# Sparse-attention, dense layer and capacity-routed experts: expert loads, splits and routing products put into a fixed sequence

## The chip, the cores and the metric

The kernel runs on one core of a Trainium2 chip. Its time is the device time of one execution, in microseconds (us). TensorE (PE) does matrix products, VectorE (DVE) and ScalarE (ACT) elementwise work, GpSimd (POOL) elementwise work and indirect transfers, SyncE (SP) starts most transfers. Each engine runs its own instructions in the order in which they stand in the program and waits on semaphores for the others.

## The reference, cut to what matters

Three parts follow one another: causal sparse attention (4 x 8 heads, 576 positions, 64 wide), a dense layer (512 to 2048 to 512 with a leaky ReLU), and an expert layer on its output `x` (2304 tokens, 512 wide). The change touches only the last:

```python
logits = x @ w_gate                       # 2304 x 8
order = np.argsort(-logits.flatten())
for idx in order:                         # greedy, by falling logit
    tok, e = (int(idx) // E, int(idx) % E)
    if assigned[tok] >= 0 or counts[e] >= cap:   # cap = 288
        continue
    assigned[tok] = e
    counts[e] += 1
for e in range(E):
    mask = assigned == e
    h = np.maximum(x[mask] @ w1[e], 0.0)
    out[mask] = h @ w2[e]
```

Every expert gets exactly 288 tokens. `w1[e]` is 512 x 1024 and `w2[e]` 1024 x 512, in float32.

## The kernel before, in words

Float32 products are made of three faster ones: each operand is split into a high part (`hi`, rounded by ACT) and the rest (`lo`, a subtraction on POOL or DVE), and hi x hi, hi x lo, lo x hi are added up in PSUM.

Attention and the first dense product come first, then `second(4)` and `second(5)`: the last two of six 384-token blocks of the second dense product (products `q`). Its rows go to a DRAM array `x2d`.

**Routing** is the generator `routes`. For each expert it has a *search* and a *list*. The search (`search`) finds the expert that fills up next and the value of its last token, in five rounds. A round compares all 2304 keys with 128 or 64 thresholds on DVE (masks `G`; rounds 0 and 3 need two), counts on PE with 18 tiny products (`cnt`), turns counts into flags on DVE (`flag`) and adds these up with one product (`tot`), whose result the next round's `G` reads. So a round is a chain DVE, PE, DVE, PE. The search ends with some thirty small DVE operations and a product `po`. The list (`tokens`) makes the expert's 288 token numbers: three one-hot masks `OQ`, `rhs`, 18 products `pi`, and `idx`. All DVE work of routing goes through the helper `Soon` and carries its line, L641.

**An expert** (`expert`) has 32 steps of 6 products `g`: 16 steps for `w1` (8 outputs `hh` by ACT and `hl` by DVE) and 16 for `w2` (4 outputs `ot`, turned back by `pot` and scattered to `out` by POOL). After every second step the routing generator moves on by one yield. `weights(k)` loads eight pieces of 512 KB (`raw`, three buffers) and splits them (`whi` on ACT, `wlo` on POOL, or on DVE for pieces 1, 5, 7). `gather(k)` fetches 288 rows of `x2d` by three indirect transfers on POOL (`xg`); PE turns them (`pet`, 12 transposes), ACT and DVE split them (`exh`, `exl`).

The order on each engine is set by a list scheduler that goes by priority and its own durations; `Soon` raises the priority of routing. In the old kernel, search k+1 and list k+1 both run during experts k-1 and k, and the gather is emitted at step 22 of expert k.

Of the kernel before, what the change touches and what calls it, by code (L numbers as in the profile page):

```python
# [7 lines left out]
F32 = mybir.dt.float32  # L8
# [18 lines left out]
def body(ctx, tc, q, k, v, w_in, w_out, w_gate, w1, w2, out):  # L27
# [617 lines left out]

    def search():
# [16 lines left out]
        for r in range(len(th)):  # L663
# [24 lines left out]
            if r in (0, 2):  # L688
                tb = rbank([128, 16], "tot")
            nc.tensor.matmul(tb[:, 8:9], units[unit][:J], f[:J], start=(r in (0, 2)), stop=True,  # L690
                             skip_group_check=True)
# [20 lines left out]
    def route(k):  # L712
# [20 lines left out]
        nc.tensor.matmul(po, tri, tot, start=True, stop=False)  # L733
# [13 lines left out]
        yield from tokens(k)  # L747

    def tokens(k):
# [4 lines left out]
        soon.scalar_tensor_tensor(s, c1[:, 0], -96.0, s, op0=OP.mult, op1=OP.add)  # L754
        soon.scalar_tensor_tensor(s, c1[:, 1], -96.0, s, op0=OP.mult, op1=OP.add)
        soon.tensor_scalar(cc[:, 0], c1[:, 0], -1.0, 1.0, op0=OP.mult, op1=OP.add)
        soon.tensor_copy(cc[:, 2], c1[:, 1])
        soon.tensor_sub(cc[:, 1], c1[:, 0], cc[:, 2])
        soon.tensor_scalar(s, s, -1.0, None, op0=OP.add)
        OQ = rtile([128, 18, 96], "OQ", BF, bufs=1)  # L760
        for i in range(0, 18, 6):
            soon.tensor_tensor(OQ[:, i:i + 6], jf[:, None, :96].to_broadcast([128, 6, 96]),
                               s[:, i:i + 6].unsqueeze(2).to_broadcast([128, 6, 96]), op=OP.is_equal)
        rhs = rtile([128, 2, 3, 18], "rhs", BF)
        soon.tensor_mul(rhs[:, 0], cc, jf[:, None, :18].to_broadcast([128, 3, 18]))
        soon.tensor_scalar(rhs[:, 1], cc, tokp, None, op0=OP.mult)
        for _ in range(4):
            yield
        pi = rbank([96, 2, 3], "pi")
        for i in range(18):  # L770
            nc.tensor.matmul(pi.rearrange("p t c -> p (t c)"), OQ[:, i], rhs[:, :, :, i].rearrange("p t c -> p (t c)"),
                             start=(i == 0), stop=(i == 17))
# [10 lines left out]
    def weights(k):  # L783
        e = nc.values_load(EXP[k][0:1, 0:1], engines=[mybir.EngineType.SP], min_val=0, max_val=7)
        W[k] = []
        for n in range(8):
            raw = POOLA[0].tile([128, 1024], F32, name="raw", tag="raw", bufs=3)
            if n < 4:
                nc.sync.dma_start(raw, w1[bass.ds(e, 1), 128 * n:128 * n + 128, :].rearrange("e p m -> (e p) m"))
            else:  # L790
                nc.sync.dma_start(raw.rearrange("p (j m) -> p j m", j=2),
                                  w2[bass.ds(e, 1), 256 * (n - 4):256 * (n - 4) + 256, :].rearrange(
                                      "e (j p) m -> p (e j) m", j=2))
            if n < 4 and k % 2:
                hi, lo = (xa.tile([128, 1024], F32R, name="w" + x, tag=f"WI{n + y}") for x, y in (("hi", 0), ("lo", 4)))
            else:
                pool, tag, bufs = (POOLB[0], "w2", 5) if n >= 4 else (POOLA[0], "w1", 4)
                hi = pool.tile([128, 1024], F32R, name="whi", tag=tag + "h", bufs=bufs)
                lo = pool.tile([128, 1024], F32R, name="wlo", tag=tag + "l", bufs=bufs)
            nc.scalar.activation(hi, raw, AF.Copy)  # L800
            (nc.vector if n in (1, 5, 7) else nc.gpsimd).tensor_sub(lo, raw, hi.bitcast(F32))  # L801
            W[k].append((hi, lo))
            yield
# [23 lines left out]
    def expert(k):  # L827
# [41 lines left out]
        def end():  # L869
            back(3, ots[3])  # L870
            put()
# [110 lines left out]
```

## Time and profile before

| what | us |
|---|---|
| three runs | 922.45, 928.96, 1975.76 |
| their median | 928.96 |
| the profiled execution | 926.83 |
| its span in the trace | 925.1 |
| PE busy in it | 860.2 (93%) |
| DVE, ACT, POOL busy | 563.3, 441.9, 471.5 |
| mean granted PE clock | 0.963 |

The page cuts the span into slices; here stretches of the expert stage are used instead, cut at each expert's first product `g` (at 627.68, 662.9, 697.05, 734.65, 773.05, 814.95, 856.5 and 885.55 us; expert 7 ends at 912.4). The last product `q` ends at 613.98. Matmuls overlap, so a busy PE is not a PE at its peak; of the clock, 1.00 is 2.4 GHz and 0.50 is 1.2 GHz.

### The profile page before, as it was taken

What the parts mean: (1) busy time and instruction counts of PE and PEld (TensorE: products, weight loads), DVE (VectorE), ACT (ScalarE), POOL (GpSimd) and SP (SyncE); (2) the same over time, 40 slices, a digit from 0 to 9 for tenths busy, and PEclk for the clock granted to TensorE, in tenths of its full rate; (3) what the DMA queues carried; (4) which work ended last, traced back from release to release, by engine and by line L of the source; (5) the groups of instructions that cost most, each with busy time, mean ns of one, the idle gap of its engine ahead of it and who ended that gap; (6) DMA issues with size and microseconds to landing.
All of it is one profiled execution on the core that took longest, in us unless ns stands there. A gap on an engine that the chain in (4) does not pass through costs nothing.

```text
span 925.1 us, 16905 instructions
## 1 busy us (share of the span) xinstructions
PE 860.2 (93%) x6274; PEld 726.1 (78%) x6274; DVE 563.3 (61%) x1543; ACT 441.9 (48%) x1095; POOL 471.5 (51%) x394
## 2 busy tenths in 40 slices
PE   7889998899999999999999999978998989897994
PEld 4777766587887888778898877658998989797994
DVE  6777889856446445554555556566877767675330
ACT  5778667464446445454455423324435434243531
POOL 3645646564555556555655445745446263426621
PEclk9789999999999999999999999987999999798997
DMA  8596554320111100100000002325356362425710
GB/s 183 142 200 157 141 144 124 119 61 5 36 26 53 43 14 2 47 1 1 35 1 1 1 1 80 114 67 177 129 154 185 102 182 95 141 92 154 213 35 26
DMA packets 86450, 80.59 MB, mean 87 GB/s; under 512 B 65376, under 2 KB 65376, under 8 KB 86368
## 3 DMA queue, kind: packets, MB, share of 16 engines
q1 hardware_dynamic: 78688, 53.30, 21.1%
q0 software_dynamic: 7680, 26.22, 9.3%
q8 instruction: 49, 0.80, 0.4%
q14 instruction: 33, 0.27, 0.1%
HBM read 70.06 MB, written 9.44 MB: 86 GB/s over the span
## 4 chain that ended last, share of the span: by engine, by line
PE 64%; DMA 10%; DVE 9%; issue 7%; POOL 4%; ACT 4%; SPq 1%; POOLq 0%; ACTq 0%; DVEq 0%
PE p L373 5%; PE p L397 5%; DMA raw<-in_moe_w_dram 4%; PE p L375 4%; PE p L374 4%; PE p L399 4%; PE p L398 4%; PE g L859 3%; PE g L860 3%; PE g L861 3%; PE p L536 2%; PE q L896 2%; PE p L538 2%; PE pS L166 2%; PE p L537 2%
## 5 line engine op out<-in xcount | busy, mean ns | idle before, releaser
L352 POOL TENSOR_TENSOR lo<-WO,hi 128x512 fp32r<-128x512 f32 x96 | 126.6, 1319 | 95.1 <-ACT hi L349 94.9
L352 POOL TENSOR_TENSOR lo<-WI,hi 128x512 fp32r<-128x512 f32 x96 | 126.9, 1323 | 90.1 <-DVE hi L351 58.3
L801 POOL TENSOR_TENSOR wlo<-raw,whi 128x1024 fp32r<-128x1024 f32 x40 | 95.8, 2410 | 113.9 <-ACT whi L800 113.3
L373 PE MATMUL p<-xh,hi 128*128 128x384 f32 x256 | 98.1, 383 | 5.5 <-DVE g L382 5.5
L349 ACT ACTIVATE hi<-WO 128x512 fp32r<-128x512 f32 x96 | 60.5, 630 | 88.2 <-PE q L898 43.7
L375 PE MATMUL p<-xh,lo 128*128 128x384 f32 x256 | 86.9, 339 | 1.4 <-POOL lo L352 1.4
L800 ACT ACTIVATE whi<-raw 128x1024 fp32r<-128x1024 f32 x64 | 66.1, 1055 | 44.4 <-DMA raw<-in_moe_w_dram 39.2
L374 PE MATMUL p<-xl,hi 128*128 128x384 f32 x256 | 86.6, 338 | 0.6 <-DVE xl L234 0.6
L397 PE MATMUL p<-hi,gh 128*128 128x512 f32 x192 | 82.8, 431 | 0.8 <-ACT gh L383 0.8
L859 PE MATMUL g<-hh,whi 128*128 128x288 f32 x256 | 81.4, 319 | 0.5 <-ACT hh L843 0.5
L860 PE MATMUL g<-hl,whi 128*128 128x288 f32 x256 | 79.0, 309 | 0.1
L861 PE MATMUL g<-hh,wlo 128*128 128x288 f32 x256 | 78.7, 307 | 0.0
L836 PE MATMUL g<-exh,whi 128*128 128x288 f32 x256 | 78.4, 307 | 0.0
L837 PE MATMUL g<-exl,whi 128*128 128x288 f32 x256 | 77.4, 303 | 0.0
L838 PE MATMUL g<-exh,wlo 128*128 128x288 f32 x256 | 77.2, 302 | 0.0
L399 PE MATMUL p<-hi,gl 128*128 128x512 f32 x192 | 75.7, 394 | 1.3 <-DVE gl L384 1.3
L159 ACT ACTIVATE sc<-sc,mx 96x128 f32<-96x128 f32 (+2 forms) x176 | 67.6, 386 | 16.6 <-DVE mx L157 16.6
L398 PE MATMUL p<-lo,gh 128*128 128x512 f32 x192 | 75.2, 392 | 0.0
L373 PEld LDWEIGHTS p<-xh,hi 128*128 128x128 f32 x256 | 48.2, 188 | 16.6 <-DVE g L382 6.8
L181 POOL TENSOR_TENSOR sc<-sc,mx 96x384 f32<-96x384 f32 (+2 forms) x64 | 52.3, 834 | 17.3 <-DVE mx L179 10.2
L381 ACT ACTIVATE g<-p 128x384 f32<-128x384 f32 x64 | 31.1, 486 | 57.0 <-PE p L375 56.7
L351 DVE CAST hi<-WI 128x512 fp32r<-128x512 f32 x59 | 26.8, 454 | 46.1 <-PE p L374 35.9
(203 smaller groups left out, 2257.5 us busy)
## 6 DMA issues: line engine op xcount, KB each, us to landing
raw<-in_moe_w_dram SPq DMA_DIRECT2D x64, 512.0 KB
wraw<-in_moe_w_in_dram POOLq DMA_DIRECT2D x16, 512.0 KB
wraw<-in_moe_w_out_dram POOLq DMA_DIRECT2D x16, 512.0 KB
rawq<-in_q_dram SPq DMA_DIRECT2D x32, 144.0 KB
rawk<-in_k_dram SPq DMA_DIRECT2D x32, 144.0 KB
x2d<-x SPq DMA_DIRECT2D x18, 256.0 KB
vt<-in_v_dram SPq DMA_DIRECT2D x16, 160.0 KB
vt<-in_v_dram SPq DMA_DIRECT2D x48, 27.0 KB
```

Source lines behind the costliest of these rows:

```text
L352: nc.gpsimd.tensor_sub(lo, src, hi.bitcast(F32))
L373: nc.tensor.matmul(p1, wh[:, cs], xh[:, c], start=(c == 0), stop=False)
L374: nc.tensor.matmul(p1, wh[:, cs], xl[:, c], start=False, stop=False)
L375: nc.tensor.matmul(p1, wl[:, cs], xh[:, c], start=False, stop=(c == 3))
L397: nc.tensor.matmul(p2[t], gh[:, s], oh, start=(f == 0), stop=False)
L398: nc.tensor.matmul(p2[t], gh[:, s], ol, start=False, stop=False)
L399: nc.tensor.matmul(p2[t], gl[:, s], oh, start=False, stop=(f == 15))
L801: (nc.vector if n in (1, 5, 7) else nc.gpsimd).tensor_sub(lo, raw, hi.bitcast(F32))
L836: nc.tensor.matmul(p, wh, xh[:, c], start=(c == 0), stop=False)
L859: nc.tensor.matmul(p, wh, hh[:, j], start=(j == 0), stop=False)
L860: nc.tensor.matmul(p, wh, hl[:, j], start=False, stop=False)
L861: nc.tensor.matmul(p, wl, hh[:, j], start=False, stop=(j == 7))
```

## The change

Four things.

1. `pin(x)` marks an instruction so that it keeps the program's order on its engine against other marked ones. Marked are the first product of each `cnt` and `pi` group, `tot`, the first `po`, `whi`, `wlo`, the gathers, and the first transpose of each `pet` group.
2. `weights` becomes `load(k, n)` and `halves(k, n)`, called at the eight steps of `CH`. A split follows its load three places later; `raw` has four buffers; piece 1 is split on POOL, no longer on DVE.
3. The list of expert k runs beside the search for k+1 (`routes`), in more and smaller steps, and a search gets 11 yields (one more in round 0). Searches are done (`FOUND`) ahead of the first load of an expert, lists (`LISTED`) ahead of the gather, which is emitted at step 16; its transposes stand at steps 24, 26, 28, 30.
4. Four pieces of expert 0 are split within `second(5)`; the rest follow.

```diff
@@ search
                 if i0 == 0:
                     yield
+                    if r == 0:
+                        yield
                 for i in range(i0, i1):
-                    nc.tensor.matmul(cnt[:J], G[:, i - i0], C[:, i], start=(i == 0), stop=(i == 17))
+                    x = nc.tensor.matmul(cnt[:J], G[:, i - i0], C[:, i], start=(i == 0), stop=(i == 17))
+                    if i == i0:
+                        pin(x)
...
@@ route / tokens
-        yield from tokens(k)
...
@@ weights -> load, halves
+    def load(k, n):
+        if n == 0:
+            W[k] = []
+            REG[k % 2] = nc.values_load(EXP[k][0:1, 0:1], engines=[mybir.EngineType.SP], min_val=0, max_val=7)
+        e = REG[k % 2]
+        raw = POOLA[0].tile([128, 1024], F32, name="raw", tag="raw", bufs=4)
...
+    def halves(k, n):
+        raw = RAWE.pop((k, n))
...
+        pin(nc.scalar.activation(hi, raw, AF.Copy))
+        pin((nc.vector if n in (5, 7) else nc.gpsimd).tensor_sub(lo, raw, hi.bitcast(F32)))
...
@@ gather
-            with tc.high_priority(2000):
-                nc.gpsimd.indirect_dma_start(out=xg[:, c], out_offset=None, in_=x2d[:, :],
-                                             in_offset=ind(IDX[k][:, c:c + 1]))
+            pin(nc.gpsimd.indirect_dma_start(out=xg[:, c], out_offset=None, in_=x2d[:, :],
+                                             in_offset=ind(IDX[k][:, c:c + 1])))
+        yield
...
@@ routes
-        for k in range(8):
-            yield from route(k)
-            ROUTED[0] = k + 1
+        T = iter(())
+        for k in range(8):
+            if k == 7:
+                for _ in T:
+                    yield
+            for _ in route(k):
+                if k and next(T, 1) == 1:
+                    LISTED[0] = k
+                yield
+            for _ in T:
+                yield
+            LISTED[0] = k
+            FOUND[0] = k + 1
+            T = tokens(k)
...
@@ the loop over experts
+    CH = {n: i for i, n in enumerate((1, 4, 7, 10, 14, 18, 22, 26))}
...
+            if n in CH:
+                c = CH[n]
+                if c < 3:
+                    halves(k, 5 + c)
+                elif k < 7:
+                    halves(k + 1, c - 3)
+                if k < 7:
+                    need(FOUND, k + 1)
+                    load(k + 1, c)
+            if k < 7:
+                if n == 16:
+                    need(LISTED, k + 1)
+                    nxt = gather(k + 1)
+                    next(nxt)
+                if n >= 24 and n % 2 == 0:
+                    next(nxt, None)
```

On DVE, the first two rounds of the search for expert 3 stood like this before, during expert 1 (`st` is the routing state, `f` the flags' sum):

```order
L641 SCALAR_TENSOR_TENSOR G<-th_5951,zero_5963,st 128x1152 x2
L844 SCALAR_TENSOR_TENSOR hl<-g_7563,hh 128x288
L641 TENSOR_SCALAR flag,f_7553<-cnt 128x8
L844 SCALAR_TENSOR_TENSOR hl<-g_7591,hh 128x288
L641 SCALAR_TENSOR_TENSOR G<-th_5953,tot,st 128x1152
L844 SCALAR_TENSOR_TENSOR hl<-g_7627,hh 128x288
L801 TENSOR_TENSOR wlo<-raw,whi 128x1024
L641 TENSOR_SCALAR flag,f_7617<-cnt 64x8
```

And now, during the last quarter of expert 0:

```order
L641 SCALAR_TENSOR_TENSOR G<-th_5951,zero_5963,st 128x1152 x2
L641 TENSOR_SCALAR c_7288<-st 128x18 x2
L641 SCALAR_TENSOR_TENSOR st<-c_7288,st 128x18
L641 TENSOR_SCALAR flag,f_7353<-cnt 128x8
L641 SCALAR_TENSOR_TENSOR st<-c_7288,st 128x18
L641 TENSOR_SCALAR st<-st 128x18
L641 TENSOR_SCALAR st<-c_7288 128x18
L641 COPY st<-c_7288 128x18
L641 TENSOR_TENSOR OQ<-jf,st 128x576
L641 SCALAR_TENSOR_TENSOR G<-th_5953,tot,st 128x1152
L641 TENSOR_TENSOR OQ<-jf,st 128x576 x2
L641 TENSOR_SCALAR flag,f_7415<-cnt 64x8
```

The list of expert 2 now stands between a round's flags and the next round's masks, and two of its `OQ` ahead of the following flags.

On PE, the same place now (the first `tot` is that of round 0; between the two marks stand the other products of round 1):

```order
L698 MATMUL tot<-f_7353,units_5957 128x1
L888 MATMUL g_7437<-hl,whi 128x288
L889 MATMUL g_7437<-hh,wlo 128x288
L689 LDWEIGHTS G
L689 MATMUL cnt<-C,G 64x8
...
L698 LDWEIGHTS units_5959
L698 MATMUL tot<-f_7415,units_5959 128x1
L838 MATMUL pet<-ident,xg 128x96 x3
L689 LDWEIGHTS G
```

Before, 14 products `g` stood between that `tot` and the next `cnt`; now 2 do, and between the following `tot` and `cnt` three transposes.

On POOL, the middle of the expert stage before:

```order
L801 TENSOR_TENSOR wlo<-raw,whi 128x1024 x5
L875 DMA out_dram<-o,idx 2304x512 x3
L809 DMA xg<-x2d,idx 96x512 x3
L801 TENSOR_TENSOR wlo<-raw,whi 128x1024 x4
L875 DMA out_dram<-o,idx 2304x512 x3
```

And now:

```order
L827 DMA xg<-x2d,idx 96x512 x3
L821 TENSOR_TENSOR wlo<-raw,whi 128x1024 x3
L869 DMA out_dram<-o,idx 2304x512 x3
L821 TENSOR_TENSOR wlo<-raw,whi 128x1024 x3
L827 DMA xg<-x2d,idx 96x512 x3
```

The pattern repeats for every expert: gather, three splits, scatter, three splits.

## Rows read from the trace of the kernel before

**Rows 1.** Busy time by stretch, expert stage: start, us, engines' busy (instructions), PEclk, DMA, GB/s.
```profile
613.98:627.68 13.70, 5.03 (x69) 4.33 (x67) 6.41 (x17) 4.06 (x6) 7.79 (x7) 0.65 0.46 144
627.68:662.90 35.22, 34.68 (x292) 33.55 (x291) 26.04 (x70) 16.08 (x29) 13.47 (x7) 0.89 0.44 136
662.90:697.05 34.15, 33.32 (x316) 31.41 (x315) 25.98 (x69) 14.79 (x28) 17.70 (x12) 1.00 0.50 159
697.05:734.65 37.60, 34.50 (x334) 32.52 (x333) 27.88 (x69) 15.79 (x29) 17.59 (x12) 1.00 0.48 144
734.65:773.05 38.40, 35.55 (x332) 33.69 (x331) 27.34 (x68) 16.06 (x29) 18.62 (x12) 0.96 0.47 141
773.05:814.95 41.90, 37.20 (x304) 35.19 (x303) 27.67 (x73) 15.90 (x28) 17.11 (x12) 0.88 0.40 130
814.95:856.50 41.55, 34.91 (x288) 33.50 (x287) 27.57 (x85) 15.14 (x28) 19.63 (x15) 0.92 0.47 141
856.50:885.55 29.05, 28.47 (x218) 28.00 (x217) 10.13 (x15) 15.07 (x29) 15.79 (x9) 1.00 0.57 172
885.55:912.40 26.85, 26.85 (x206) 26.82 (x205) 6.24 (x9) 6.78 (x17) 4.86 (x4) 1.00 0.08 23
```

**Rows 2.** Waits of PE, 627.7 to 913 us: total, times, longest.
```profile
PE pet L819 <- DMA xg<-x2d,idx: 7.1, 2, 4.2
PE cnt L683 <- DVE G L641: 4.5, 4, 2.4
PE pi L771 <- DVE rhs L641: 3.3, 4, 1.6
```

**Rows 3.** Busy time by stretch, after the longest of these waits.
```profile
843.40:850.20 6.80, 5.39 (x27) 5.34 (x28) 1.70 (x5) 1.78 (x5) 3.80 (x2) 0.50 0.78 194
```

**Rows 4.** DVE by line, 627.7 to 856.5 us: busy, mean ns, idle before.
```profile
L801 DVE TENSOR_TENSOR wlo<-raw,whi 128x1024 fp32r<-128x1024 f32 x19 | 31.4, 1654 | 5.2 <-ACT whi L800 5.2
L641 DVE SCALAR_TENSOR_TENSOR G<-th,tot,st 128x1152 bf16<-128x1152 f32 x19 | 26.5, 1414 | 4.2 <-PE tot L690 4.2
...
L641 DVE TENSOR_TENSOR OQ<-jf,st 128x576 bf16<-128x576 f32 x18 | 12.5, 748 | 0.1
...
L641 DVE SCALAR_TENSOR_TENSOR idx<-ip 96x3 int32<-96x3 f32 x6 | 4.1, 676 | 0.0
...
L641 DVE TENSOR_SCALAR_CACHE_REDUCE flag<-cnt 64x8 bf16<-64x8 f32 x14 | 2.2, 157 | 9.2 <-PE cnt L683 8.6 <-PE g L838 0.6
L641 DVE SCALAR_TENSOR_TENSOR st<-c,st 128x18 f32<-128x18 f32 x12 | 2.1, 179 | 0.1
```

**Rows 5.** The chain that ended last: start, us, what.
```profile
614.63 2.74 DMA x2d<-x
...
648.47 0.66 PE cnt L683 x18
...
661.57 0.80 PE pi L771 x18
```

**Rows 6.** PE in order of time, expert 3: start, us, engine, line, idle before.
```profile
750.14 0.30 PE L859 MATMUL g<-hh,whi 128*128 128x288 f32 x1
750.28 0.29 PE L860 MATMUL g<-hl,whi 128*128 128x288 f32 x1
753.01 0.38 PE L683 MATMUL cnt<-C,G 128*128 128x8 bf16 x9 [2.44 <-DVE G L641]
```

**Rows 7.** POOL in order of time, a gather in expert 4.
```profile
791.77 2.39 POOL L801 TENSOR_TENSOR wlo<-raw,whi 128x1024 fp32r<-128x1024 f32 x1 [0.89 <-ACT whi L800]
794.32 0.93 POOL L809 DMA_INDIRECT xg<-x2d,idx  x1 [0.16 <-issue]
...
796.79 0.92 POOL L809 DMA_INDIRECT xg<-x2d,idx  x1 [0.30 <-issue]
```

**Rows 8.** PE in order of time, the transposes of that gather.
```profile
799.76 1.72 PE L819 MATMUL pet<-ident,xg 96*128 96x96 f32 x5 [2.92 <-DMA xg<-x2d,idx]
```

**Rows 9.** DVE and POOL in order of time, start of the expert stage.
```profile
613.32 0.69 DVE L902 COPY x<-q 128x512 f32<-128x512 f32 x1 [1.08 <-PE q L898]
...
618.35 1.01 POOL L809 DMA_INDIRECT xg<-x2d,idx  x1 [6.56 <-DMA x2d<-x]
```

More of the change, by code (lines that the diff above doesn't have):

```diff
@@ L644, in body, with pin @@
     soon = Soon()
+    def pin(x):
+        tc.keep_in_program_order(x[0] if isinstance(x, tuple) else x)
     def search():
@@ L781, in ind @@
         return bass.IndirectOffsetOnAxis(ap=ap, axis=0)
[L783 to L803, printed above, removed]
@@ new lines, in body @@
+    REG, RAWE = [None, None], {}
+    def halves(k, n):
+        raw = RAWE.pop((k, n))
+        if n < 4 and k % 2:
+            hi, lo = (xa.tile([128, 1024], F32R, name="w" + x, tag=f"WI{n + y}") for x, y in (("hi", 0), ("lo", 4)))
+        else:
+            pool, tag, bufs = (POOLB[0], "w2", 5) if n >= 4 else (POOLA[0], "w1", 4)
+            hi = pool.tile([128, 1024], F32R, name="whi", tag=tag + "h", bufs=bufs)
+            lo = pool.tile([128, 1024], F32R, name="wlo", tag=tag + "l", bufs=bufs)
+        pin(nc.scalar.activation(hi, raw, AF.Copy))
+        pin((nc.vector if n in (5, 7) else nc.gpsimd).tensor_sub(lo, raw, hi.bitcast(F32)))
+        W[k].append((hi, lo))
@@ L844, in expert, with put @@
             nc.vector.scalar_tensor_tensor(hl[:, j], p, 0.0, hh[:, j].bitcast(F32), op0=OP.max, op1=OP.subtract)
-        o = e2.tile([96, 3, DM], F32, name="o", tag="o", bufs=2)
+        o = e2.tile([96, 3, DM], F32, name="o", tag="o")
+        def put(r):
+            st = nc.gpsimd.indirect_dma_start(out=out, out_offset=ind(IDX[k][:, r:r + 1]), in_=o[:, r],
+                                              in_offset=None)
+            for x in scat:
+                tc.declare_no_dep(st.ins, x.ins, reason="each token has one expert and one place")
+            scat.append(st)
         def back(c, ot):
@@ L870, in end @@
             back(3, ots[3])
-            put()
-        def put():
             for r in range(3):
-                st = nc.gpsimd.indirect_dma_start(out=out, out_offset=ind(IDX[k][:, r:r + 1]), in_=o[:, r],
-                                                  in_offset=None)
-                for x in scat:
-                    tc.declare_no_dep(st.ins, x.ins, reason="each token has one expert and one place")
-                scat.append(st)
+                put(r)
         if k < 7:
@@ L921, in body @@
     POOLA[0] = ctx.enter_context(tc.tile_pool(name="pa", bufs=1, reuse_waits="tile"))
-    need(0)
-    wx = weights(0)
     for f, _ in enumerate(second(5)):
         next(R, None)
-        if f % 4 == 1:
-            next(wx)
+        if f == 3:
+            need(FOUND, 0)
+            for n in range(4):
+                load(0, n)
+        if 7 <= f < 15 and f % 2:
+            halves(0, (f - 7) // 2)
+        if f == 13:
+            load(0, 4)
+            load(0, 5)
     right.close()
     POOLB[0] = ctx.enter_context(tc.tile_pool(name="pbx", bufs=1, reuse_waits="tile", side="right"))
-    for _ in gather(0):
-        pass
-    for _ in wx:
-        pass
+    need(LISTED, 0)
+    with tc.high_priority(4000):
+        for _ in gather(0):
+            pass
+    load(0, 6)
+    halves(0, 4)
+    load(0, 7)
+    CH = {n: i for i, n in enumerate((1, 4, 7, 10, 14, 18, 22, 26))}
     for k in range(8):
@@ L938, in body @@
                 next(R, None)
[L939 to L951 removed]
+            if n in CH:
[14 more added lines that the diff above has]
+                    next(nxt, None)
+        for _ in nxt:
+            pass
 _INS = ['q', 'k', 'v', 'moe_w_in', 'moe_w_out', 'moe2_w_gate', 'moe2_w1', 'moe2_w2']
```

56 lines of the change are left out of this document (30 added, 26 removed).

## The prediction

> **What bounds the kernel now.** I read first the busy time by stretch, because the change touches only routing and experts, and within the second dense product it moves little. In [rows 1] the reader is to see three kinds of expert. Experts 6 and 7 have no routing left: 29.05 us and 26.85 us, PE without a gap. Expert 1 carries one search and takes 34.15, of which PE is idle for 0.83. Experts 2 to 5 take 37.6 to 41.9. So a plain expert costs 29.05, a search adds about 4.3 of PE time (34.15 - 0.83 - 29.05), and a list adds its 18 products, 0.80 [rows 5]. What remains is loss, of two sorts. PE idle in experts 0 to 5, stretch less busy time, is 0.54 + 0.83 + 3.1 + 2.85 + 4.7 + 6.64 = 18.7 us. And the granted clock: one minus PEclk, times the stretch, gives 3.9 + 0 + 0 + 1.5 + 5.0 + 3.3 = 13.7 us.
>
> Then the waits of PE [rows 2]: transposes for a gather 7.1, `cnt` for masks 4.5, `pi` for `rhs` 3.3. No wait for `whi` or `wlo` is among them: weights are late for ACT and POOL, not for PE, so an earlier load gains nothing by itself. After the longest wait the clock stood at its lower level for 6.8 us [rows 3]; that is how one wait of 4.2 us costs 4.2 + 3.4.
>
> DVE is what PE waits for most often, though it is busy for only 26 to 28 us of each routed expert [rows 1]. The reason is order: in [rows 6] PE stands 2.44 us ahead of a `cnt`, because its masks stood on DVE behind `hl` operations, which waited for ACT.
>
> **The change, part by part.** The order of the changed kernel shows where routing goes. After expert 0's first product there remain 23 rounds in both kernels (search 2 from its third round, searches 3 to 6). Before they lie in experts 0 to 5, now in 0 to 3. Lists: six before, seven now, since list 1 comes later. Expert 0 gets 6.5 rounds and two lists, expert 1 6.5 and one, experts 2 and 3 five and one each, expert 4 two lists, 5 to 7 nothing.
>
> *PE's own work in experts 0 to 3.* 4 x 29.05 = 116.2; 23 rounds are 4.6 searches at 4.3 = 19.8; five lists at 0.8 = 4.0. Together 140.0.
>
> *DVE's work there.* Experts 0 to 5 held 162.5 us of it [rows 1]. Two of them lose their routing but keep what expert 6 shows, 10.1 each; four splits of piece 1 at 1.65 [rows 4] go to POOL; one list comes in, three `OQ` at 0.75 and small operations, about 4. 162.5 - 20.3 - 6.6 + 4 = 139.6. So DVE, with much slack before, now has as much to do as PE, and a chain that goes to and fro between the two cannot keep both full. This is the core of the forecast.
>
> *The tight places.* I walked the four experts with these durations: a mask 1.41, an `OQ` 0.75, a small list operation 0.18, flags 0.24 (0.157 and the reading of the sum) [rows 4], 18 counts 0.66 [rows 5], a product 0.13 (26.85 over the 206 instructions of expert 7 [rows 1]; [rows 6] has two 0.14 apart), three transposes 0.37.
> - End of expert 0, search 3, the place shown in the change. After the flags of round 0 DVE runs four small operations (0.72), an `OQ` (0.75) and a mask (1.41), 2.9 in all; PE has a `tot` and two products, 0.4: wait 2.4. The next flags stand behind two `OQ`: 1.50 + 0.24 - 0.66 = 1.1. Then 0.43 + 1.41 against three transposes: 1.5. `pi` waits for flags and `rhs`: 0.7. Sum 5.7.
> - Expert 1, search 4: round 2 has one product as cover (1.84 - 0.13 = 1.7); round 3 none at all, so both its masks are waited for, 1.4 + 1.1; `po` 0.8; flags behind `idx` 0.4. Sum 5.4.
> - Expert 2, search 5: `po` 1.0, rounds 0 and 1 0.8, a split (1.65) ahead of round 2's mask 1.0, rounds 3 and 4 with little between 2.7. Sum 5.5.
> - Expert 3, search 6: more cover, two splits in the chain; 3.0.
>
> Together 19.6, against the 18.7 that go. From below: half of it, if DVE catches up between; from above 28, if each mask and split is as late as the one in [rows 6]. I take 19.6, since before the same counting (14 and 10 products of cover) gives expert 1 no wait, as [rows 1] has it.
>
> *The clock.* The fall at the start stays (0.65 in the first stretch, 3.9 us lost in expert 0). The falls of experts 3 to 5 go with their waits. I put one fall like [rows 3], worth 3.4, behind each of the clusters of experts 0 and 1: 3.9 + 6.8 = 10.7. Bounds: 3.9, and 17.5 with four falls.
>
> So experts 0 to 3 take 140.0 + 19.6 + 10.7 = 170.3. Expert 4 takes 29.05 + 1.6, expert 5 29.05. Experts 0 to 5: 230.0, against 228.8 in [rows 1]: **+1.2**. The routing moves forward by two experts and pays there what it saves later.
>
> *The gather.* Emitted at step 16 instead of 22, with its list ready one search earlier, it should end the wait of 7.1. It stands on POOL behind the split of step 14. From that step: `whi` some 1.1, split 2.39, the three issues 2.5 from first to third, then 3.0 until transposes ran (796.79 to 799.76) [rows 7, 8]: 9.0. PE reaches the first transposes 66 products and three back-transposes later, 8.9. So it just fits, and in experts 4 to 6, where no routing slows PE, it may be late by some tenths: **+1.0** for all; bounds 0 and 13 (4.2 each).
>
> *The splits.* POOL has six of 2.4 us and six indirect issues of 1.2 per expert, 22 of 29 us: hidden as long as raw data comes in time, which the fourth buffer and three places of lead serve. If that cover goes, see the second rival. In `second(5)` POOL gets a fourth split between its `lo` of the products `q`, PE waiting for these: 0 to 2.4, I take **+0.5**.
>
> *The start.* The copy of one `q` result on DVE ended with the last product (613.32 + 0.69 against 613.98); now it stands behind masks and `OQ` of search 2, about 2.4 us later, and the write to `x2d` (2.74 [rows 5]) and the gather (618.35 [rows 9]) with it. Against that, only three gathers go out there instead of six and twelve transposes follow each other; before, counts stood between, and the first product came 13.7 after the last `q` [rows 1]. Bounds -3 and +2.4; I take **+0.5**, nearer the row on the copy. Expert 7 and what follows it are unchanged.
>
> **Sum.** On the profiled execution, 926.83 (span 925.1): + 1.2 + 1.0 + 0.5 + 0.5 = 930.0. The median of the runs shown is 928.96, 0.2% above the profiled one. Within 2%, about what a measurement of this kernel can tell from no change, means 908 to 945 here.
>
> **Rivals.**
> - *DVE hides after all* (chance 0.22). The waits in the clusters mostly vanish, because DVE is ahead when PE arrives. Experts 0 to 3 then take PE's 140 plus the start's 3.9 and a remainder of 3 to 6, about 148 instead of 170: 930 - 22 = 908, and 900 to 904 if the start gains as well. For it: the change takes `hl` and splits out of ACT's waits for raw data (5.2 us of DVE's idle time [rows 4]), the cause in [rows 6]; expert 1 before ran a whole search at 0.83 of idle time. Against it: one list more in each search, and places with one product of cover or none. The Trainium skill, page "Perfetto Trace Analysis", section "Identifying the Most-Contended Engine", ranks engines by occupancy and would have PE's queue alone set the time, which is this rival; [rows 6] has PE waiting for a DVE that is busy for under three quarters of the stretch, so the trace only half agrees.
> - *POOL's fixed order makes the gather late* (0.13), slower. Splits, gathers and scatters can no longer pass each other on POOL. If a piece comes late, its split holds the gather behind it, and PE meets its transposes too early. It decides at the point where the third issue starts less than 3.0 us before PE's first transpose [rows 7, 8]. Price per expert as in [rows 2, 3]: 4.2 + 3.4 = 7.6; in three of the seven gathers behind the first it is 23, less the 1.0 counted: 952; in two, 944. For it: the margin above is nil. Against it: the loads run further ahead than before.
> - *The pins change little* (0.05): if the marked instructions were late in the old order anyway, everything stays at 925 to 930. The order speaks against it, since searches do end two experts earlier.
>
> **How the numbers follow.** My forecast has 0.60: 930, by its own bounds 914 to 943 (half the cluster waits and only one fall at the low end; 28 us of waits or one late gather at the high end). The range reaches into the first rival down to 905 and into the second up to 946, leaving out a little over a tenth below and under a tenth above. Faster by over 2%: most of the first rival and a little of my own low end, 0.24. Slower: the second rival and the high end, 0.15. Within 2%: 0.61.
>
> **What would show it.** In the profile after: experts 4 to 6 near 29 to 31 us each, with PEclk 1.00 (else the gather term is wrong); experts 0 to 2 at 40 to 46 us with PE waits for `G`, `flag` and `rhs` of about 5.5 each, and DVE over 80% busy there; no PE wait for `xg` over 1 us after the first; first product `g` 13 to 15 us after the last `q`. If experts 0 to 3 take under 155 us together, the tight places were counted too dear, and the first rival holds. If PE waits for `xg` in several experts, the second does. A PE wait for `whi` or `wlo` would be outside all of this.

## The result and the profile after

| | median us | runs from to |
|---|---|---|
| before, same chip, five runs | 925.70 | 919.85 to 1975.76 |
| after, five runs | 934.59 | 934.03 to 935.44 |

The ratio is 1.0112, 95% interval 1.0067 to 1.0158 (the run of 1975.76 was disturbed and is left out of it): slower by about 1%, within the 2% forecast as no change. The profiled execution of the changed kernel took 934.59, its span is 932.8, the mean granted clock 0.956 (0.963 before).

Busy time by stretch of the changed kernel, with the columns of [rows 1]: the start (last `q` to first `g`), then experts 0 to 7, each cut at its first `g`.

```profile
616.40:628.97 12.57, 3.31 (x33) 2.67 (x32) 5.28 (x14) 1.53 (x4) 2.85 (x3) 0.62 0.32 110
628.97:676.49 47.52, 42.67 (x387) 40.19 (x385) 31.75 (x89) 16.32 (x29) 19.43 (x10) 0.81 0.37 113
676.49:725.24 48.75, 39.79 (x357) 37.46 (x354) 35.27 (x87) 15.27 (x28) 19.79 (x12) 0.86 0.34 111
725.24:764.47 39.23, 36.97 (x338) 35.26 (x335) 28.90 (x93) 15.13 (x28) 20.13 (x12) 0.91 0.46 138
764.47:798.61 34.14, 34.11 (x336) 32.40 (x333) 26.90 (x79) 16.02 (x30) 20.13 (x12) 1.00 0.50 156
798.61:831.45 32.84, 30.63 (x257) 29.82 (x256) 19.48 (x63) 15.55 (x28) 21.20 (x12) 1.00 0.51 169
831.45:863.13 31.68, 30.17 (x219) 29.57 (x217) 7.78 (x15) 15.73 (x28) 20.68 (x12) 0.95 0.54 171
863.13:893.36 30.23, 28.63 (x220) 28.05 (x217) 7.76 (x15) 15.67 (x28) 20.72 (x12) 1.00 0.52 162
893.36:920.15 26.79, 26.79 (x206) 26.75 (x204) 5.94 (x11) 9.29 (x19) 6.15 (x4) 1.00 0.08 23
```

The reader is to see the loss change place. Before, experts 0 and 1 took 35.2 and 34.2 and experts 4 and 5 nearly 42 each [rows 1]; now 0 and 1 take 47.5 and 48.8, and 4 to 6 are near a plain expert. Step by step the span went from 925.05 to 932.82, +7.8:

| part | after less before |
|---|---|
| up to the first `q` of `second(5)`, which the change leaves alone | +0.75 |
| `second(5)`, from its first `q` to the start of its last (41.50 to 43.17) | +1.67 |
| start (13.70 to 12.57) | -1.13 |
| experts 0 to 5 (228.82 to 234.16) | +5.34 |
| expert 6 (29.05 to 30.23) | +1.18 |
| expert 7 and what follows | -0.04 |

The changed kernel differs in one thing more than the four listed: the output tile `o` has one buffer instead of two. No wait for a free `o` shows in the trace.

What PE waited for from 627 to 925 us (total, times, longest), to be laid beside [rows 2]:

```profile
PE cnt L689 <- DVE G L641: 9.4, 7, 2.2
PE po L741 <- DVE tot L641: 5.6, 2, 4.8
PE pet L838 <- DMA xg<-x2d,idx: 4.9, 9, 1.0
PE tot L698 <- DVE flag L641: 1.2, 3, 0.7
PE pi L780 <- DVE rhs L641: 1.0, 2, 0.6
```

Waits for masks doubled (4.5 before), two waits for a gather of up to 4.2 became nine of at most 1.0, and a wait for `po` as long as 4.8 is new (1.3 before). As before, PE nowhere waits for `whi` or `wlo`.

The start: the copy of the last `x` rows on DVE, and the transposes that wait for the first gather, of the changed kernel (compare [rows 9]):

```profile
618.02 0.68 DVE L924 COPY x<-q 128x512 f32<-128x512 f32 x1
```
```profile
624.87 0.42 PE L838 MATMUL pet<-ident,xg 96*128 96x96 f32 x1 [6.56 <-DMA xg<-x2d,idx]
```

The copy ends 2.3 after the last `q` (616.40), where it ended with it before; even so the first `g` comes 1.1 sooner behind that `q`.

The cluster at the end of expert 0, PE in order of time (the place whose order stands in the section on the change; only `cnt`, `tot`, `pet` and `pi` are shown, the products between are left out):

```profile
659.34 0.18 PE L698 MATMUL tot<-f,units 128*128 128x1 bf16 x1
...
662.12 0.73 PE L689 MATMUL cnt<-C,G 128*64 128x8 bf16 x18 [2.24 <-DVE G L641]
663.53 0.16 PE L698 MATMUL tot<-f,units 64*128 64x1 bf16 x1 [0.67 <-DVE flag L641]
663.62 0.70 PE L838 MATMUL pet<-ident,xg 96*128 96x96 f32 x3
...
665.70 1.12 PE L689 MATMUL cnt<-C,G 128*64 128x8 bf16 x18 [1.38 <-DVE G L641]
...
667.38 0.81 PE L780 MATMUL pi<-rhs,OQ 128*96 128x6 bf16 x9 [0.56 <-DVE rhs L641]
```

Four waits in a row, 4.85 together, for the reason walked in the prediction: DVE puts small list operations, an `OQ` and a mask between a `tot` and the next `cnt`, and PE has two products or three transposes to do meanwhile. This can be counted over the whole expert stage. Of the 22 places between a `tot` and the next `cnt`, five have at most three products or transposes, and PE waited at each of them: 2.24 and 1.38 here, 1.68 and 1.51 in expert 1, 1.51 in expert 2. The other 17 have at least 13, and PE waited at none. (Cover is not all: before, with at least 13 everywhere, PE still waited at three, up to 2.44, for the order on DVE [rows 6].) The last group of counts above ran at the low clock (18 counts took 1.12 instead of 0.73). Busy time by stretch, for the two falls of the clock behind the clusters of experts 0 and 1:

```profile
663.71:673.95 10.24, 8.30 (x63) 7.75 (x64) 5.77 (x14) 2.63 (x5) 2.34 (x1) 0.50 0.18 53
691.02:697.85 6.83, 5.36 (x24) 5.36 (x24) 4.51 (x15) 1.49 (x3) 0.25 (x1) 0.50 0.56 203
```

The second fall follows the longest wait, which was not walked. DVE, POOL and PE in order of time in expert 1:

```profile
686.03 6.33 DVE L821 TENSOR_TENSOR wlo<-raw,whi 128x1024 fp32r<-128x1024 f32 x1
692.29 0.15 DVE L641 CAST tot<-st 128x2 bf16<-128x2 f32 x1
```
```profile
685.66 0.92 POOL L869 DMA_INDIRECT out_dram<-o,idx  x1 [0.30 <-issue]
686.59 4.68 POOL L821 TENSOR_TENSOR wlo<-raw,whi 128x1024 fp32r<-128x1024 f32 x2
```
```profile
692.49 0.16 PE L741 MATMUL po<-tot,tri 128*128 128x2 bf16 x1 [4.85 <-DVE tot L641]
```

A split that DVE does in 1.22 elsewhere took 6.33 here, and ended 1.1 after the second of two splits on POOL (686.59 + 4.68 = 691.27). It began 0.56 ahead of the first of them, while POOL issued a scatter. Behind it on DVE stood the cast that `po` needs. No idle time stands before it on DVE: the time is inside the operation. All DVE splits from 627 us on, duration in ns (min/median/max), before and then after:

```profile
L801 DVE TENSOR_TENSOR wlo<-raw,whi x23: 1206/1226/3317, 630.8 to 886.1; 128x1024 fp32r<-128x1024 f32 x23
```
```profile
L821 DVE TENSOR_TENSOR wlo<-raw,whi x16: 1207/1218/6332, 633.7 to 901.2; 128x1024 fp32r<-128x1024 f32 x16
```

So the mean of 1654 in [rows 4] was no operation's time: most took 1.22, and eight of 23 took 1.95 to 3.32. The prediction used the mean, which hides that there are two kinds of split.

### The profile page after: what moved, and what is told of

Same layout as the page of the kernel before. It is cut to its first block, busy times and chain, and to the rows that moved or that the text cites. A ratio compares the mean times of both kernels' runs of the same rounds, so it can differ in the third digit from the quotient of the medians.

```text
span 932.8 us, 16884 instructions
## 1 busy us (share of the span) xinstructions
PE 862.8 (92%) x6274; PEld 729.5 (78%) x6274; DVE 545.3 (58%) x1535; ACT 443.0 (47%) x1095; POOL 492.0 (53%) x402
## 5 line engine op out<-in xcount | busy, mean ns | idle before, releaser
L821 POOL TENSOR_TENSOR wlo<-raw,whi 128x1024 fp32r<-128x1024 f32 x48 | 115.8, 2429 | 56.0 <-ACT whi L820 49.5
L159 ACT ACTIVATE sc<-sc,mx 96x128 f32<-96x128 f32 (+2 forms) x176 | 67.6, 387 | 17.1 <-DVE mx L157 17.1
L869 POOL DMA_INDIRECT out_dram<-o,idx x24 | 25.2, 1049 | 87.9 <-ACT o L879 51.0
L181 POOL TENSOR_TENSOR sc<-sc,mx 96x384 f32<-96x384 f32 (+2 forms) x64 | 52.5, 838 | 18.4 <-DVE mx L179 11.7
```

Source lines behind the costliest of these rows:

```text
L821: pin((nc.vector if n in (5, 7) else nc.gpsimd).tensor_sub(lo, raw, hi.bitcast(F32)))
```

## The experiments

Three causes stood to be told apart: the tight places (dependent products on PE with too little between them, since two lists and more than one search fall into an expert); the list beside the search by itself; and DVE being held by POOL. The base of each edit is the changed kernel. Each ratio is against runs of the kernel before on the same chip, whose median differed from chip to chip (924 to 934), so ratios are compared, not medians. One thing varies between profiled executions with no edit near it: the fall of the clock at the start, ahead of the first `g` and into expert 0, lasted 17.07 us after the change and 10.24 in gather12, whose edit comes later in the program. That is worth 2 to 3 us in expert 0, so sums over experts 1 to 6 are given where it matters.

**gather12: the gather at step 12.**

```diff
-                if n == 16:
+                if n == 12:
                     need(LISTED, k + 1)
```

> One part of the change is moved: the gather is emitted at step 12 of an expert, ahead of the split of step 14, instead of at step 16. Theory 1 (the change loses in three places: routing packed into fewer experts, a gather that comes late behind the split on POOL, a fuller POOL in second(5)): the waits of PE for xg after the first gather (0.84, 1.52 and 1.42 us in experts 4, 5, 6, and one clock fall of 3.4 us) go, experts 5 and 6 take 29 us each instead of 31.6 and 30.1; 934.6 becomes 930 to 931. Theory 2 (the whole loss is one subtraction on DVE that took 6.33 us beside POOL, in expert 1): no change within 1 us, if that subtraction stays as it is.

Measured: 936.30, ratio 1.0079 (1.0039 to 1.0119). Waits for `xg` behind the first are gone, and experts 5 and 6 took 27.90 and 27.88 instead of 31.59 and 30.14 (from first to last `g`), 6.0 us less. The time did not fall with it. That is the total which Theory 2 expected, but it came about by gains and losses that cancel. The moved gather moved POOL's splits, and these met another DVE split. DVE, then POOL, in order of time, expert 2:

```profile
741.96 3.94 DVE L821 TENSOR_TENSOR wlo<-raw,whi 128x1024 fp32r<-128x1024 f32 x1
```
```profile
740.09 4.71 POOL L821 TENSOR_TENSOR wlo<-raw,whi 128x1024 fp32r<-128x1024 f32 x2
```

PE waited 2.16 for that `wlo`, the clock fell for 10.2 us, and expert 2 took 44.1 instead of 39.1; expert 4 lost 2.5 to an `idx` that took 4.19 instead of 0.15. The expert stage, from first `g` to the end of expert 7, took 291.3 against 291.2; experts 1 to 6 took 219.13 against 216.87, the rest being the shorter fall of the clock at the start. The late gather was a real cost of about 6 us, and its gain was given back where the chain is tight.

**pace13: 13 routing steps per expert instead of 16,** none at steps 24, 26 and 28. A search yields 13 times (11 in its rounds, two ahead of `po`), so each expert carries just one.

```diff
-            if n % 2 == 0:
+            if n % 2 == 0 and n not in (24, 26, 28):
```

> Routing is slowed: it does not move on at steps 24, 26 and 28 of an expert, so 13 yields an expert, one search each, and the 23 rounds lie in experts 0 to 4. In the order 10 to 14 products now stand between a tot and its next cnt nearly everywhere. Theory 1 (tight places): the waits of PE for G, flag, rhs in experts 0 to 2 (11 us) and most of their clock falls (12 us) go; expert 0 some 38 us, experts 1 to 4 34 to 36; 912 to 918. Theory 2 (one slow subtraction of 6.33 us on DVE beside POOL, with the wait for po and the clock fall behind it, 8.2 us): 926 if it does not recur, 935 if it does. Theory 3 (the list beside the next search loads DVE too much, wherever the rounds lie): waits of 2 to 3 us stay in each of experts 1 to 4; 926 to 934.

Measured: 911.05, ratio 0.9801 (0.9738 to 0.9864). Busy time by stretch, experts 0 and 1 (2 and 3 are alike, 35.2 and 36.0), then PE's waits from 624 us to the end:

```profile
629.65:667.28 37.63, 37.02 (x331) 34.91 (x330) 26.41 (x77) 16.15 (x29) 19.37 (x10) 0.91 0.49 143
667.28:703.17 35.89, 34.46 (x335) 32.53 (x333) 28.20 (x80) 15.48 (x29) 20.83 (x12) 1.00 0.50 151
```
```profile
PE pet L838 <- DMA xg<-x2d,idx: 13.0, 15, 6.6
PE tot L698 <- DVE flag L641: 1.8, 7, 0.3
```

No wait for `G` or `po` is left, and after the start (0.91 in expert 0) the clock stays at 1.00 to expert 5, though each search has its list beside it and DVE is as busy as before. Experts 0 to 3 went from 169.6 to 144.7. All 22 places between a `tot` and the next `cnt` now have at least 14 products or transposes. But pace13 removes a second thing too: its longest DVE split took 2.42, so the 6.33 did not come again. By poolall below that is worth some 6 us, and with it alone Theory 2 expected 926; the greater part of the 25 is left to the tight places. The list beside the search is not the cost, as long as PE has products between one dependent group and the next.

**pace13np: pace13 without the marks on `cnt`, `tot`, `po` and `pi`.**

```diff
-                    if i == i0:
-                        pin(x)
...
-            pin(nc.tensor.matmul(tb[:, 8:9], units[unit][:J], f[:J], start=(r in (0, 2)), stop=True,
-                                 skip_group_check=True))
+            nc.tensor.matmul(tb[:, 8:9], units[unit][:J], f[:J], start=(r in (0, 2)), stop=True,
+                             skip_group_check=True)
```

> The slower routing without the marks on cnt, tot, pi and po (those on splits, gathers and transposes stay). It undoes one part, the fixed place of the routing products. In the order, rounds 2 and 3 of search 2 now stand ahead of the first transposes of expert 0, and places with 3 products of cover or none return at the start of expert 0; from the end of expert 1 on the order is nearly that with marks. Theory 1 (a wait comes from few products between tot and cnt, whoever put them there): 2 to 5 us of waits for G and flag at the start of expert 0, partly inside the wait for the gather there, little elsewhere; 911 to 916. Rival (the marks themselves cost, since marked products cannot be passed): 905 or less.

Measured: 908.23, ratio 0.9774 (0.9684 to 0.9865), not to be told from pace13; the median lies between the two ranges and decides nothing. PE's waits for `G` and `flag` came ahead of the first `g` as expected (1.52, 0.67, 0.27), inside the wait for the gather; elsewhere `flag` cost up to 1.54. These marks are worth nothing that can be measured, with this pace.

**seqlist: each list behind its own search again,** as before the change, everything else as changed.

```diff
-            for _ in route(k):
-                if k and next(T, 1) == 1:
-                    LISTED[0] = k
-                yield
...
+            yield from route(k)
             FOUND[0] = k + 1
-            T = tokens(k)
+            yield from tokens(k)
+            LISTED[0] = k + 1
```

> One part is undone: the list of an expert follows its own search again instead of standing beside the next search; marks, loads, splits and gather stay as changed. Theory 1 (what costs is how few products stand between the steps of a round): in the order every expert from 0 to 4 now has a place near its end with 1 to 5 products and 3 transposes as cover for two masks, so 3 to 4 us of waits in each of five experts and clock falls behind some: 930 to 940. Theory 3 (the list beside the search is what costs): the waits for G, flag and rhs fall by half or more; 922 to 927.

Measured: 936.11, ratio 1.0082 (1.0051 to 1.0113): the same as the change. PE's waits, 624 us to the end:

```profile
PE cnt L689 <- DVE G L641: 11.6, 8, 1.6
PE g L888 <- DVE hl L865: 4.5, 4, 1.7
```

The waits are shorter but more, and experts 1 to 5 took 39.95, 40.26, 43.93, 40.19 and 37.74 (from first to last `g`), with a fall of the clock of 6.8 us in each, two in expert 3. In each of experts 1 to 4 one place has a single product and one has three transposes, and PE waited 1.3 and 1.6 there, as Theory 1 had it. One behind the other, search and list need 13 and 7 steps, so routing lasts through expert 5; side by side they crowd into experts 0 and 1. In the parts that the change touches the list beside the search is a gain: without it the expert stage took 299.6 instead of 291.2, `second(5)` and the start 2.3 and 1.5 less than after the change. Of this no more than a few us can show, and the medians do not tell the two apart. It is not what made the change no faster.

**dve1: piece 1 split on DVE again, as before.**

```diff
-        pin((nc.vector if n in (5, 7) else nc.gpsimd).tensor_sub(lo, raw, hi.bitcast(F32)))
+        pin((nc.vector if n in (1, 5, 7) else nc.gpsimd).tensor_sub(lo, raw, hi.bitcast(F32)))
```

> One part is undone: piece 1 of each expert is split on DVE again. Theory 1: POOL is less full in second(5), its two waits for lo (0.54 and 1.16 us) shrink to what the kernel before has, -0.5 to -1; DVE has one more operation of 1.2 to 1.6 us per expert in its chain in experts 0 to 3, +2 to +5; in all 934 to 939. Theory 2 (POOL's trains of splits are what holds up DVE's own splits): with five splits instead of six per expert on POOL the 6.33 us operation shrinks to under 3 us, the wait for po of 4.85 us and its clock fall go: 926 to 930.

Measured: 941.81, ratio 1.0125 (1.0071 to 1.0179). The long split of expert 1 stayed (6.34), against Theory 2. A second came, and PE's `pi` waited 3.94 for the `rhs` behind it:

```profile
825.54 4.71 DVE L821 TENSOR_TENSOR wlo<-raw,whi 128x1024 fp32r<-128x1024 f32 x1
```

The expert stage took 294.7 instead of 291.2, within Theory 1's +2 to +5. `second(5)` took 44.24, no less than with piece 1 on POOL (43.17), where Theory 1 expected a gain. DVE has the split there instead, so this alone does not clear POOL; seqlist does, with the same four splits on POOL in a `second(5)` of 40.88.

**poolall: no split on DVE at all.**

```diff
-        pin((nc.vector if n in (5, 7) else nc.gpsimd).tensor_sub(lo, raw, hi.bitcast(F32)))
+        pin(nc.gpsimd.tensor_sub(lo, raw, hi.bitcast(F32)))
```

> The changed kernel with pieces 5 and 7 also split on POOL, so that DVE has no split at all. The question is what the 6.33 us that one split held DVE in expert 1 was worth. Theory A (the late po is the split's): the wait of 4.85 for tot goes to about 1, and with it the clock's fall behind it (6.8 us at half speed, worth 3.4), so expert 1 comes from 48.7 to about 41.5 and the median from 934.6 to about 926; no DVE operation of 1 us or less takes over 3 us there. POOL then has eight splits of 2.4 and six issues of 1.2, some 26 us per expert, so a gather may come later by up to 2.4 in experts 4 to 6: up to +7 against it, 926 to 933. Theory B (it is the list and the nearness of the products alone; the split only fills time in which DVE would have waited anyway): the wait for po stays over 3 and the median stays at 932 to 938. Rival C (POOL becomes the bound): PE waits for wlo, the median is 940 or more.

Measured: 939.78, ratio 1.0184 (1.0128 to 1.0241), an interval that overlaps with that of the change. Expert 1 did as Theory A expects: 42.35 instead of 48.67, no wait for `po`. The total did not follow: the expert stage took 293.2 instead of 291.2 (the other 3.6 of the profiled execution lay ahead of it, the last `q` ending at 620.0 instead of 616.4). PE nowhere waited for `wlo`, so Rival C is out. Gathers came later (PE waits of 2.03 and 2.75 for `xg` in experts 5 and 6), and in expert 4 POOL held other operations of DVE. Busy time of expert 1, then DVE (only operations over 1.2 us), POOL and PE in order of time in expert 4:

```profile
679.18:721.61 42.43, 39.08 (x357) 36.69 (x354) 28.06 (x85) 15.37 (x28) 24.53 (x14) 0.88 0.42 128
```
```profile
796.86 2.28 DVE L641 COPY ab<-unl 128x18 f32<-128x18 f32 x1
800.13 2.08 DVE L641 TENSOR_TENSOR OQ<-jf,st 128x576 bf16<-128x576 f32 x3
804.65 4.19 DVE L641 SCALAR_TENSOR_TENSOR idx<-ip 96x3 int32<-96x3 f32 x1
```
```profile
796.71 2.40 POOL L821 TENSOR_TENSOR wlo<-raw,whi 128x1024 fp32r<-128x1024 f32 x1 [5.68 <-ACT whi L820]
...
804.14 4.67 POOL L821 TENSOR_TENSOR wlo<-raw,whi 128x1024 fp32r<-128x1024 f32 x2
```
```profile
809.33 0.16 PE L741 MATMUL po<-tot,tri 128*128 128x2 bf16 x1 [3.70 <-DVE tot L641]
```

An `idx` of 96 x 3 elements, 0.15 when nothing holds it, ended with POOL's second split (804.65 + 4.19 = 808.84 against 804.14 + 4.67 = 808.81), and a copy of 128 x 18 with POOL's single one (799.14 against 799.11). Experts 4 to 6 took 103.6 instead of 94.5: -6.3 in expert 1, +9.1 here.

**port: the hold by itself.** A kernel that leaves out all of the reference's computation: about 0.2 us after POOL begins 0, 1, 2 or 4 subtractions of 128 x 1024, DVE runs one operation behind two small ones.

```diff
+        for i in range(n):
+            nc.gpsimd.tensor_sub(w, raw, g)
+        nc.vector.tensor_scalar(spin[:, :64], g[:, :64], 1.0, None, op0=OP.mult)
+        nc.vector.tensor_scalar(spin[:, 64:256], g[:, :192], 1.0, None, op0=OP.mult)
+        nc.vector.tensor_sub(d, raw, g)                    # or, second operand from PSUM:
+        nc.vector.tensor_sub(d[:, :512], pb, g[:, :512])   # or, one operand:
+        nc.vector.tensor_scalar(d, g, 2.0, None, op0=OP.mult)
```

> Nothing of the reference is computed: the disputed cost is measured by itself. A train of 0, 1, 2 or 4 subtractions (128x1024) runs on POOL; a little later DVE runs one operation: with two operands in SBUF (as wlo), with one in PSUM and one in SBUF (as hl, exl, G; half as wide), or with one operand in SBUF. Theory A (DVE's operation with two SBUF operands waits until POOL's train is over): 1.2 us alone, about 2.4, 4.8 and 9.6 more or less the start with 1, 2 and 4; the one with PSUM keeps its time. Theory B (they share, each slowed): 1.2 alone and about twice that in all other cases; POOL's own operations get longer. Theory C (the 6.33 us had another cause): no difference.

Measured, DVE in order of time: two operands in SBUF with 0, 2 and 4 subtractions on POOL; one operand in PSUM with 4 (0.68 with 0 too); one operand in SBUF with 0 and 4 (2.83 with 1 and 2 too). Then POOL's train of 4 beside the first kind and beside the PSUM kind.

```profile
7.24 1.22 DVE L55 TENSOR_TENSOR dtwo<-raw,g 128x1024 f32<-128x1024 f32 x1
...
18.07 3.36 DVE L55 TENSOR_TENSOR dtwo<-raw,g 128x1024 f32<-128x1024 f32 x1
...
26.13 3.36 DVE L55 TENSOR_TENSOR dtwo<-raw,g 128x1024 f32<-128x1024 f32 x1
...
53.43 0.68 DVE L57 TENSOR_TENSOR dpsum<-pb,g 128x512 f32<-128x512 f32 x1
...
65.09 0.69 DVE L59 TENSOR_SCALAR done<-g 128x1024 f32<-128x1024 f32 x1
...
82.37 2.83 DVE L59 TENSOR_SCALAR done<-g 128x1024 f32<-128x1024 f32 x1
```
```profile
25.96 10.33 POOL L49 TENSOR_TENSOR wpool<-raw,g 128x1024 f32<-128x1024 f32 x4 [2.32 <-ACT g L46]
...
53.26 9.35 POOL L49 TENSOR_TENSOR wpool<-raw,g 128x1024 f32<-128x1024 f32 x4 [2.32 <-ACT g L46]
```

Here the DVE operation waits until the POOL operation that is running ends, and then goes first, POOL's train being longer by 1.0 for it (10.33 against 9.35); in port it waits for one, however long the train, so Theory A holds for a train of one alone. In the whole kernel it can wait for more (pace13g12 below). (Beside a train of one, the small operation ahead was held, 2.40 instead of 0.26, and the subtraction then took 1.21.) With an operand in PSUM nothing waits. It is a wait, not a shared rate as in Theory B: the loss is the same 2.14 (3.36 - 1.22, 2.83 - 0.69) for an operation of 1.22 and one of 0.69. The Trainium skill, page "GPSIMD Engine Reference", section "1. Specifications", says that GpSimd shares its SBUF interfaces with VectorE and that DVE instructions in a 2-port mode or with two SBUF inputs contend. The split and the case with PSUM agree with it. But the masks `G` and the `OQ` of the kernel, which read two SBUF operands too, kept 1.41 and 0.75 in every instance beside POOL (the three `OQ` above, 2.08, end to end), so here the rule names too many.

**pace13g12: both, 13 steps and the gather at step 12.** The edits are those of pace13 and gather12 together.

> The slower routing (no step at 24, 26, 28) and the gather at step 12 together. Theory A (the late gather costs what PE waits for xg, and the earlier gather gained nothing in the first trial only because it pushed two DVE splits into POOL's trains, 3.9 and 4.2 us): with the slower routing, where DVE has cover, the waits for xg (6.3 us in 14 pieces) go and nothing comes back; experts 5 and 6 take 28 to 29 us; 3 to 6 us less than the slower routing alone, 905 to 908. Theory B (an earlier gather only moves the wait from PE to POOL's splits): within 1 us of the slower routing alone.

Measured: 907.84, ratio 0.9764 (0.9686 to 0.9842). Waits for `xg` behind the first are gone again; in their place came two for masks (0.64 and 0.65, experts 1 and 2) and two for `exl` (1.59 and 1.34, experts 4 and 5). The last two come from holds by POOL once more: ahead of the first, a copy of 128 x 18 took 4.05 instead of 0.17, through the end of one subtraction on POOL and the whole of the next; ahead of the second, an `idx` was held through four. DVE, then POOL, expert 5:

```profile
816.87 8.35 DVE L641 SCALAR_TENSOR_TENSOR idx<-ip 96x3 int32<-96x3 f32 x1
```
```profile
815.80 9.40 POOL L821 TENSOR_TENSOR wlo<-raw,whi 128x1024 fp32r<-128x1024 f32 x4
```

The `idx` ended with the fourth (816.87 + 8.35 = 825.22 against 815.80 + 9.40 = 825.20), and POOL's subtractions kept their 2.4 each; the same came again in best (8.38). So the moved splits still hold DVE, but with cover between the products a hold of 8.35 cost PE 1.34, and the clock did not fall. The expert stage took 260.6, against 267.2 in pace13, but 3.0 of that is expert 0, where the fall of the clock at the start lasted 10.2 us instead of 17.1. Experts 1 to 6 took 199.19 against 202.79: some 3.6 us are kept, not 6. The ratios of the two overlap, so the runs alone show neither theory.

**best: pace13g12, and the copies of the last `x` rows on ACT.**

```diff
-                    (nc.vector.tensor_copy if t % 2 else nc.scalar.copy)(x2, q_)
+                    nc.scalar.copy(x2, q_)
```

> The slower routing, the gather at step 12, and all three last copies of x on ACT instead of one on DVE, where it stood behind masks and one-hot masks of search 2. If that copy holds up the write to x2d and so the first gather by 2 us or more, as I worked out, the time from the last product q to expert 0's first product falls from 12.6 to 10 or 11 us: 902 to 906. If the write is bound by ACT's or the queue's own order: within 1 us of the second run's.

Measured: 904.89, ratio 0.9706 (0.9628 to 0.9785), not to be told from pace13g12 by the ratio. The start took 10.98 instead of 12.57, and `second(5)` 42.03 instead of 43.17; PE's wait for the first gather, which was 6.56 after the change:

```profile
622.97 0.42 PE L838 MATMUL pet<-ident,xg 96*128 96x96 f32 x1 [5.06 <-DMA xg<-x2d,idx]
```

**bestpool: best without splits on DVE.** Edit as in poolall.

> The fastest version so far (13 yields per expert, gather at step 12, copies of the last blocks on ACT; 904.9) with pieces 5 and 7 also split on POOL. If DVE's splits cost only where the products stand close, there is nothing left to gain: 902 to 908. If they still delay the chain: 898 to 902. If POOL becomes the bound with the gather between its splits: 910 to 920, with PE waits for wlo or xg.

Measured: 894.41, ratio 0.9702 (0.9651 to 0.9753): in the ratio the same as best, the lower median is the chip's (before: 924.48 there). In the profiled executions experts 1 to 6 took 193.1, against 199.9 in best and 199.2 in pace13g12, and the waits of best for `flag`, `G` and `exl` (2.0, 2.0 and 2.9) are gone. So the splits on DVE still cost some 6 us there, as the second case expects, which the ratios are too coarse to show. Busy time, experts 0 and 1:

```profile
622.16:659.10 36.94, 36.94 (x331) 35.16 (x330) 26.86 (x76) 16.11 (x28) 24.06 (x12) 0.89 0.46 145
659.10:693.04 33.94, 33.94 (x335) 32.37 (x333) 25.23 (x78) 15.62 (x28) 24.46 (x14) 1.00 0.52 157
```

PE has no gap left in a routed expert. The same edit that made the expert stage 2.0 us longer in poolall makes it shorter here, and POOL's 24.5 us per expert keep PE waiting for no `wlo`. Both versions beat the kernel before by 3%.

## Why the prediction was right, and where it was not

The forecast of no change (930) held: 934.6, +1.1% against the runs beside it. The interval leaves out no change at all, so this is a small loss, of 7.8 us in the span where the sum had 3.2. Its mechanism held as well: routing moved forward by two experts and paid there, in PE waits of the walked kind, what it saved later; pace13 removes these waits (and the long split with them) and ends 2% below the kernel before. Of the signs it named, four missed: experts 0 and 1 (47.5 and 48.8, for 40 to 46), DVE's share, the start, and PEclk in expert 5 (0.95). By its steps:

- **Experts 0 to 3** came out at 169.6, predicted 170.3, but by terms that cancel: that it is right to 0.7 us is luck. PE's idle time was 4.85 + 8.96 + 2.26 + 0.03 = 16.1 (19.6). Behind the first `g` the clock was at its lower level for 7.4 + 10.2 + 6.8 + 6.8 + 6.8 = 38.1 us; in 32.8 of these PE was busy, and half of that, 16.4, was lost (10.7). PE's own work is then, by difference, 137.1 (140.0); the plain expert of 29.05 that it was built from was not without a gap, as the prediction has it, but held 0.58 of idle time [rows 1].
- **Expert 0's cluster** was walked at 2.4, 1.1, 1.5, 0.7 and measured 2.24, 0.67, 1.38, 0.56. Expert 1's rounds 2 and 3 were walked at 1.7, 1.4 and 1.1 and measured 1.68, 1.51 and 0.92. Experts 2 and 3 were counted too dear: 2.3 and nothing, for 5.5 and 3.0; DVE caught up there, as the lower bound had it.
- **"`po` 0.8" in expert 1** is the term that was mis-sized: 4.85, with a fall of the clock behind it (6.8 us at half). It was priced by the products between; it was made by a DVE split of 6.33, held beside POOL. poolall, without splits on DVE, shows its worth: 6.3 us in that expert.
- **DVE "as much to do as PE", over 80% busy:** wrong. It was 139.6 in the sum; measured 31.75 + 35.27 + 28.90 + 26.90 = 122.8, or 67 to 74% of experts 0 to 2. The sum had all lists in experts 0 to 3, but expert 4, where the prediction itself put two, kept DVE busy for 19.48, against 7.78 in expert 5: 11.7 of the 16.8 too much. It also carried over POOL's delays of before (31.4 for 19 splits [rows 4], 1.22 each without). And waiting to and fro leaves both engines idle. The waits rest on the order, not on DVE's load: pace13 has DVE at 79% of expert 1 with few waits.
- **The gather, +1.0:** too low. That it "just fits" was right to a microsecond (waits of at most 1.0), but in experts 4 to 6 they add up to 0.84, 0.93 + 0.31 + 0.28 and 1.02 + 0.40, 3.8 in all, and a fall of the clock of 3.4 us adds 1.7: 5.5. gather12 gave back 6.0 in experts 5 and 6. The waits of 4.2 did go. Not forecast at all were the waits in expert 4 for `po` (0.77) and `pi` (0.42).
- **`second(5)`, +0.5:** +1.67. POOL's split, named as the cause, is not it: seqlist has the same four splits on POOL there and took 40.88, with 90 `cnt` products and no `po`. After the change one more round of search 2 stands there (108 `cnt` instead of 90). With the copies of `x` off DVE it took 42.03 (best). How the +1.67 divides between these is not shown.
- **The start, +0.5:** -1.1. The copy did come late as walked (it ended 2.3 after the last `q`), but the start was shorter all the same; that fewer gathers and transposes without counts between were worth more is argued from the order, not tested. best, which takes the copy off DVE, gains another 1.6.
- **The rivals.** That DVE hides after all did not happen here; it is what happens with three steps less per expert. POOL's fixed order made the gather late in three experts, which was that rival's sign, but by tenths and not by 4.2: 5.5 us in all, not 15 or 23. That the change does little is excluded by the stretches.

What stays open: port has a DVE operation wait for one POOL operation, and so it was with the longest splits before the change (3.32) and in pace13 (2.42). The 6.33 of the changed kernel, the 3.94 of gather12 and the 4.19 of `idx` spanned two splits on POOL, the 8.35 of `idx` in pace13g12 four. Why DVE did not get in between them was not found.

## What to carry to other kernels

When two engines work in a chain to and fro, look at how much independent work stands between one link and the next on the waiting engine; here the busy share of either told little, and moving the chain earlier only helps if that cover comes along. Set the pace so that one link fits each slot, and only then move transfers and splits: the same edit of the gather changed experts 1 to 6 by +2.3 us at 16 steps and by -3.6 at 13. Read the longest and the median of a group, not its mean: a mean well above the median (1.65 and 1.23 here) was a second kind of event.

## What was not expected of the hardware

- A DVE operation that reads SBUF can wait inside its own duration for a running POOL operation: in port 1.22 to 3.36 for a split and 0.69 to 2.83 for one with a single operand. In the kernel it waited through up to four POOL operations in a row: 0.15 to 8.35 for an `idx` of 96 x 3. No wait on a semaphore shows. Masks, `OQ`, `hl` and `exl` (the last two read PSUM) kept their time.
- The clock fell to its lower level even behind small waits: at 854.9 for 3.4 us, after waits of 0.93, 0.31 and 0.28 in expert 5; at 691.0 for 6.8 us, during the wait of 4.85; at 663.7 for 10.2 us, after waits of 2.24 and 0.67. In pace13's searches, with waits of 0.3 in PE, it did not fall; nor did it after the waits of 1.59 and 1.34 in pace13g12. The length of the wait just before a fall does not settle it.
